# A state-space layer's kernel: the sums of two neighbouring sets made in one visit, and the order of its first stage written anew

## The chip, the cores and the metric

The kernel runs on one core of one Trainium2 chip. A core has five engines that each work through a list of instructions of their own: TensorE (PE in the profile; its weight loads are PEld), VectorE (DVE), ScalarE (ACT), GpSimd (POOL) and SyncE (SP, which here issues DMA transfers). They wait for one another by semaphores. The metric is the time of one execution on the device in microseconds (us), and lower is better. TensorE accumulates into PSUM, whose banks hold 512 numbers of 32 bits for each of 128 partitions in this kernel; the other tiles lie in SBUF, 128 partitions as well.

## The reference

One layer on 2048 tokens of 512 channels. `u` is normalised, then goes two ways: through a state-space convolution, and through an FFN (512 to 1792 to 512, GELU) whose output gates the first.

```python
xn = _layernorm(u)
# convolution: per channel d a kernel K[d, l] of 2048 taps, from 128 complex states
dt = exp(log_dt)[:, None];  logdA = dt * (A_re + 1j * A_im);  dB = dt * (B_re + 1j * B_im)
P = exp(logdA[:, :, None] * arange(L))
K = einsum("dn,dnl,dn->dl", C_re + 1j * C_im, P, dB).real
y = irfft(rfft(pad(xn)) * rfft(pad(K)))[:L] + xn * Dskip
# gate
h = gelu(einsum("bsd,df->bsf", xn, w1) + b1)
g = silu(einsum("bsf,fd->bsd", h, w2) + b2)
return u + y * g
```

## The kernel before

There are two stages. The first, up to about 394 us, is the projection stage: the layer norm, the whole FFN and the making of the kernel K. The second does the convolution as a transform in two steps with matmuls, and multiplies by the gate. The change lies in the first.

**The FFN** is 56 steps: eight passes of seven steps (four blocks of 512 tokens, each in two halves of the 1792 hidden rows). x, the weights and the hidden layer are each split in a high and a low part, and three products are summed: `first_half` (L243; L250 to L252) makes a hidden tile `f` in six matmuls a call, two calls a step; `gate` (L262) takes the GELU on ACT (`hf`); `gate_high` (L267) casts it to the high part `hh` on ACT; `ffn_rest` (L273) makes the low part `hl = hf - hh` on DVE; `second_part` (L279; L289 to L291) adds three products to one of four accumulators `z`, four calls a step. Weights are loaded by SP (`stage_first`, `stage_second`) and split by `split` (high parts on ACT, low parts `w1l`, `w2l` on DVE, L235, or on GpSimd). The layer norm's blocks are transposed by TensorE into `xT` (L361), into the buffers of `f` where the token is TF, and split by ACT and DVE into `xh` and `xl` (L376).

**The kernel K** is made in 32 sets of 16 channels. For each set `gen_phase` (L593) computes the angles of half the set by one matmul into `ph` (one bank), twice; `gen_round` (on ACT, L601, or on DVE, L603, by a flag) and `gen_wrap` (DVE, L607) reduce them to one turn in `ra`; `gen_size` (GpSimd, L616 and L619) builds the magnitudes `mm` by repeated products; `gen_sin` (ACT, L627 to L630) takes sine and cosine; `gen_tables` (DVE, L642 to L649) multiplies them into the tables `e1` and `e2`, which have two buffers each; `gen_sum` (L657) contracts e1 with e2 over the 128 states on PE, 32 small matmuls (64 records in the profile) into one half of the bank `kg`; `gen_out` copies it on ACT to `ko` (two buffers); `gen_keep` stores it by SP to `kgd`.

**What sets the order.** A table written out by hand, `ORDER`, is read token by token (the loop at L1101): each token names one of the actions above with its arguments, and calling it appends its instructions to the engines' lists. So an engine does its own instructions in the table's order, and between engines only semaphores decide. F.5.0 is first_half of step 5, its first half; G, H, R, S are gate, gate_high, ffn_rest and second_part; A, B, C, Z, N, E, Q, U, UD are gen_phase, gen_round, gen_wrap, gen_size, gen_sin, gen_tables, gen_sum, gen_out, gen_keep, the first number being the set (B with a third argument runs on the other engine); KL loads a set's inputs; W, WB and WS load and split the weights of a step; P is one step in the preparation of the parameters; TF, TH, TL transpose and split a block; D loads `dsk` and `fc` for the second stage.

Of the kernel before, what the change touches and what calls it, by code (L numbers as in the profile page):

```python
# [53 lines left out]
LS.4.0 B.0.0.1 TH.2.1 TL.2.0 C.0.0 WS.6.0 S.2.2 S.2.3 H.4 TF.3.0 A.0.1 KL.1.1 WS.5.2 S.3.0 LS.5.1 WS.6.1
Z.0 B.0.1 P.0 P.1 TH.3.0 S.3.1 C.0.1 S.3.2 A.1.0 N.0.0 TL.2.1 S.3.3 KL.2.0 LD.2 TL.3.0 WS.6.2 B.1.0.1
C.1.0 R.4 F.5.0 TF.3.1 Z.1 LD.3 LS.4.1 N.0.1 A.1.1 B.1.1.1 F.5.1 S.4.0 WS.5.3.1 TH.3.1.1 C.1.1 G.5 S.4.1
E.0.0 S.4.2 S.4.3 E.0.1 TL.3.1 F.6.0 H.5 N.1.0 R.5 F.6.1 LR.4 N.1.1 F.7.0 E.0.2 G.6 A.2.0 B.2.0.1 S.5.0
KL.2.1 LC.5 H.6 F.7.1 S.5.1 P.1 LC.4 C.2.0 WS.6.3 LK.0 F.8.0 S.5.2 A.2.1 G.7 KL.3.0 H.7 B.2.1 P.1 F.8.1
R.6 G.8 KL.3.1 C.2.1 N.2.0 S.5.3 F.9.0 E.1.0 N.2.1 Q.0 A.3.0 S.6.0 S.6.1 S.6.2 F.9.1 Z.2 E.1.1 R.7 U.0
E.1.2 P.1 LD.5 B.3.0.1 LD.4 C.3.0 O.0.0 TF.4.0 KL.4.0 Q.1 Z.3 O.0.1 H.8 S.6.3 TH.4.0 O.0.3 G.9 A.3.1  # L60
S.7.0 TL.4.0 B.3.1.1 P.1 H.9 S.7.1 C.3.1 O.0.2 KL.4.1 TF.4.1 UD.0 LL.6 TH.4.1 R.8 F.10.0 F.10.1 E.2.0
S.7.2 S.7.3 N.3.0 E.2.1 A.4.0 TL.4.1 P.1 S.8.0 R.9 KL.5.0 U.1 E.2.2 N.3.1 B.4.0.1 G.10 OK.0 S.8.1 F.11.0
E.3.0 F.11.1 S.8.2 C.4.0 A.4.1 S.8.3 Q.2 G.11 B.4.1 H.10 UD.1 TF.5.0 E.3.1 E.3.2 LK.1 F.12.0 H.11 TH.5.0
C.4.1 A.5.0 KL.6.0 LS.6.0 F.12.1 B.5.0.1 S.9.0 S.9.1 R.10 N.4.0 G.12 S.9.2 TL.5.0 TF.5.1 P.1 N.4.1 C.5.0
KL.5.1 S.9.3 F.13.0 A.5.1 U.2 TH.5.1 F.13.1 R.11 S.10.0 P.1 B.5.1 Z.4 P.1 P.1 Q.3 C.5.1 N.5.0 TL.5.1
S.10.1 P.1 E.4.0 P.1 UD.2 U.3 F.14.0 N.5.1 H.12 E.4.1 S.10.2 KL.6.1 UD.3 S.10.3 R.12 E.4.2 Z.5 G.13 A.6.0
S.11.0 S.11.1 F.14.1 H.13 LK.2 E.5.0 R.13 E.5.1 LL.7 S.11.2 S.11.3 B.6.0.1 C.6.0 Q.4 Z.6 S.12.0 G.14
A.6.1 KL.7.0 F.15.0 E.5.2 P.1 S.12.1 LS.7.0 B.6.1 LS.7.1 F.15.1 P.2 C.6.1 S.12.2 A.7.0 S.12.3 G.15 LS.6.1
F.16.0 B.7.0 C.7.0 LR.6 N.6.0 A.7.1 S.13.0 LC.6 KL.8.0 S.13.1 U.4 H.14 R.14 P.1 H.15 F.16.1 N.6.1 LC.7
P.2 UD.4 E.6.0 B.7.1 R.15 S.13.2 LD.6 KL.7.1 C.7.1 F.17.0 Z.7 S.13.3 F.17.1 G.16 TF.6.0 O.1.0 O.1.2 Q.5  # L70
A.8.0 E.6.1 G.17 TF.7.0 S.14.0 TH.6.0 P.2 TH.7.0 E.6.2 O.1.1 U.5 O.1.3 H.16 KL.8.1 TL.6.0 TL.7.0 B.8.0
N.7.0 Z.8 S.14.1 S.14.2 N.7.1 S.14.3 F.18.0 OK.1 UD.5 C.8.0 TF.6.1 A.8.1 P.2 Q.6 F.18.1 S.15.0 B.8.1.1
R.16 TH.6.1 S.15.1 C.8.1 S.15.2 U.6 KL.9.0 S.15.3 E.7.0 H.17 E.7.1 S.16.0 W.7 S.16.1 G.18 WB.7 A.9.0
KL.9.1 F.19.0 F.19.1 R.17 E.7.2 B.9.0 TL.6.1 N.8.0 S.16.2 W.8 LD.7 S.16.3 N.8.1 G.19 S.17.0 TF.7.1 C.9.0
A.9.1 E.8.0 P.2 H.18 KL.10.0 TH.7.1 E.8.1 Q.7 B.9.1.1 UD.6 C.9.1 KL.10.1 H.19 D S.17.1 S.17.2 A.10.0
E.8.2 S.17.3 N.9.0 WB.8 F.20.0 TL.7.1 P.2 F.20.1 U.7 KL.11.0 N.9.1 R.18 Z.9 B.10.0 S.18.0 C.10.0 E.9.0
A.10.1 Q.8 G.20 F.21.0 XL.0 W.9 S.18.1 B.10.1 C.10.1 KL.12.0 N.10.0 E.9.1 N.10.1 WB.9 S.18.2 E.9.2 R.19
S.18.3 W.10 F.21.1 A.11.0 F.22.0 U.8 B.11.0 C.11.0 S.19.0 KL.11.1 G.21 H.20 S.19.1 A.11.1 S.19.2 UD.7
Z.10 B.11.1 P.2 P.2 F.22.1 UD.8 LK.3 S.19.3 R.20 F.23.0 WB.10 G.22 C.11.1 E.10.0 N.11.0 S.20.0 Z.11
A.12.0 F.23.1 N.11.1 S.20.1 Q.9 H.21 O.2.0 S.20.2 E.10.1 E.10.2 B.12.0 KL.12.1 F.24.0 H.22 C.12.0 A.12.1  # L80
# [1126 lines left out]
```

## Time and profile before

| | us |
|---|---|
| median of three runs | 548.02 |
| lowest and highest run | 547.81, 549.68 |
| the profiled execution | 548.29 |
| its span, first to last instruction | 546.5 |
| PE, DVE, ACT, POOL busy in it | 526.9, 463.9, 394.5, 279.1 |

The span is divided among the engines, and every row of the profile is a group of instructions of one line: its engine, what it writes and reads, its count, the busy time in all and the mean of one, and the idle time ahead with what ended it. Busy times of the engines overlap. Matmuls are pipelined: one lasts longer than the time until the next starts, so what a piece of PE's work costs is read from the starts in the timeline. The granted clock of TensorE stands in the tables by stretch, 1.00 being full speed; its mean over the span is 0.996.

### The profile page before, as it was taken

To read this page: it belongs to the slowest core of one execution; us is meant where nothing else is said; L and a number is where in the kernel's file an instruction comes from. 1 tells how busy PE (TensorE), PEld (TensorE's weight loads), DVE (VectorE), ACT (ScalarE), POOL (GpSimd) and SP (SyncE) were. 2 spreads that over 40 slices of the span, in tenths; PEclk is the share of its full clock that TensorE was granted. 3 is DMA by queue.
4 is the path that set the end of the run, shared out by engine and by line. 5 is a ranking of instruction groups with operands and counts; after the bars stand their busy time and mean duration, and the time that the engine had idled before them with its cause. 6 is when DMAs were issued, how large, how long until landed. Compare 5 with 4: busy or idle time off the path is not lost.

```text
span 546.5 us, 16626 instructions
## 1 busy us (share of the span) xinstructions
PE 526.9 (96%) x6999; PEld 421.2 (77%) x6999; DVE 463.9 (85%) x736; ACT 394.5 (72%) x570; POOL 279.1 (51%) x385
## 2 busy tenths in 40 slices
PE   8898999999999999999999999999999999999993
PEld 7666787778776777777777777777789998997971
DVE  6899989999999889999888797789557688787896
ACT  3777998898987899959799777889664573652430
POOL 5648379358968559996854296356301001203031
PEclk9999999999999999999999999999999999999998
DMA  8937526744385172837038412913547749361562
GB/s 228 315 124 227 196 83 221 237 150 146 121 245 180 33 237 90 270 102 198 18 110 263 123 47 84 188 45 103 204 160 221 136 127 189 120 194 67 182 208 93
DMA packets 88391, 85.85 MB, mean 157 GB/s; under 512 B 42134, under 2 KB 65050, under 8 KB 87292
## 3 DMA queue, kind: packets, MB, share of 16 engines
q1 hardware_dynamic: 79248, 66.43, 41.6%
q0 software_dynamic: 8768, 17.83, 10.6%
q8 instruction: 55, 0.90, 0.7%
q10 hardware_dynamic: 300, 0.53, 0.3%
q14 instruction: 20, 0.16, 0.1%
HBM read 51.22 MB, written 33.55 MB: 155 GB/s over the span
## 4 chain that ended last, share of the span: by engine, by line
PE 76%; DVE 17%; issue 2%; ACT 1%; POOL 1%; DMA 1%; DVEq 0%; ACTq 0%; POOLq 0%
PE s L913 11%; PE z L289 8%; PE z L290 7%; PE z L291 7%; PE f L250 7%; PE f L252 7%; PE f L251 7%; PE s L891 6%; PE sa L949 6%; PE kg L657 5%; PE ph L593 2%; DVE hl L276 2%; DVE ra L607 2%; DVE e L646 1%; PE y L989 1%
## 5 line engine op out<-in xcount | busy, mean ns | idle before, releaser
L619 POOL TENSOR_TENSOR mm<-mm,rc 128x32 f32<-128x32 f32 (+4 forms) x150 | 115.4, 769 | 11.8
L289 PE MATMUL z<-w2h,hh 128*128 128x512 f32 x224 | 97.8, 437 | 0.0
L250 PE MATMUL f<-xh,w1h 128*128 128x512 f32 x220 | 91.4, 416 | 0.0
L291 PE MATMUL z<-w2h,hl 128*128 128x512 f32 x224 | 88.4, 395 | 0.3 <-DVE hl L276 0.3
L252 PE MATMUL f<-xh,w1l 128*128 128x512 f32 x220 | 87.1, 396 | 1.7 <-DVE w1l L235 1.7
L290 PE MATMUL z<-w2l,hh 128*128 128x512 f32 x224 | 88.6, 395 | 0.0
L251 PE MATMUL f<-xl,w1h 128*128 128x512 f32 x220 | 86.7, 394 | 0.0
L913 PE MATMUL s<-X,mc 64*64 64x128 f32 x1536 | 60.4, 273 | 0.2 <-issue 0.2
L930 DVE TENSOR_TENSOR t<-s,uh 128x512 f32<-128x512 f32 x64 | 41.0, 684 | 22.8 <-ACT uh L921 22.6
L276 DVE TENSOR_TENSOR hl<-hf,hh 128x512 fp32r<-128x512 f32 x56 | 52.9, 948 | 4.6 <-ACT hh L270 4.6
L616 POOL COPY mm<-rc 128x32 f32<-128x32 f32 x30 | 13.4, 446 | 77.7 <-DVE e L649 53.4
L264 ACT ACTIVATE hf<-f,b1s 128x512 f32<-128x512 f32 x56 | 38.2, 688 | 20.4 <-DVE hl L276 11.7
L252 PEld LDWEIGHTS f<-xh,w1l 128*128 128x128 f32 x220 | 41.3, 188 | 12.9 <-DVE w1l L235 3.0
L289 PEld LDWEIGHTS z<-w2h,hh 128*128 128x128 f32 x224 | 42.5, 190 | 10.5 <-issue 1.0
L291 PEld LDWEIGHTS z<-w2h,hl 128*128 128x128 f32 x224 | 42.1, 188 | 10.7 <-DVE hl L276 0.7
L607 DVE SCALAR_TENSOR_TENSOR ra<-ra,ph 128x512 f32<-128x512 f32 x64 | 43.6, 681 | 7.5 <-ACT ra L601 6.5
L913 PEld LDWEIGHTS s<-X,mc 64*64 64x64 f32 x1536 | 44.5, 133 | 5.8 <-issue 1.7
L290 PEld LDWEIGHTS z<-w2l,hh 128*128 128x128 f32 x224 | 42.3, 189 | 8.3 <-DVE w2l L235 0.2
L250 PEld LDWEIGHTS f<-xh,w1h 128*128 128x128 f32 x220 | 41.5, 189 | 9.2 <-ACT hf L264 0.2
L251 PEld LDWEIGHTS f<-xl,w1h 128*128 128x128 f32 x220 | 41.4, 188 | 9.0
L921 ACT COPY uh<-s 128x512 f32<-128x512 f32 x32 | 18.7, 586 | 38.3 <-PE s L913 18.4
L642 DVE TENSOR_TENSOR e<-mm,ra 128x1024 f32<-128x1024 f32 x32 | 42.0, 1311 | 4.7 <-POOL pr_h L524 2.4
(184 smaller groups left out, 1161.1 us busy)
## 6 DMA issues: line engine op xcount, KB each, us to landing
x<-in_A_u_dram SPq DMA_DIRECT2D x8, 512.0 KB
xs<-x SPq DMA_DIRECT2D x8, 512.0 KB
xt_h<-xh POOLq DMA_DIRECT2D x4, 1024.0 KB, 5.5
xt_l<-xl POOLq DMA_DIRECT2D x4, 1024.0 KB, 7.6
kgd<-ko SPq DMA_DIRECT2D x32, 128.0 KB
za<-zo SPq DMA_DIRECT2D x4, 1024.0 KB
xh<-xt_h POOLq DMA_DIRECT2D x4, 1024.0 KB, 6.1
xl<-xt_l POOLq DMA_DIRECT2D x4, 1024.0 KB, 10.1
```

What stands on the lines that cost most here:

```text
L250: PE.matmul(p, wh[:, k, :], xh[:, k, :], start=(k == 0), stop=False)
L251: PE.matmul(p, wh[:, k, :], xl[:, k, :], start=False, stop=False)
L252: PE.matmul(p, wl[:, k, :], xh[:, k, :], start=False, stop=(k == KD - 1))
L276: V.tensor_sub(hl, hf, hh)
L289: PE.matmul(z, hh[:, s], wh, start=(f0 == 0 and not rows), stop=False)
L290: PE.matmul(z, hh[:, s], wl, start=False, stop=False)
L291: PE.matmul(z, hl[:, s], wh, start=False, stop=(f0 == FA - 1))
L607: V.scalar_tensor_tensor(ra[:, 0, c], ra[:, 1, c], MAGIC, p, op0=ALU.subtract, op1=ALU.subtract)
L619: GP.tensor_mul(mv[:, :, 0:3:2, w:2 * w], mv[:, :, 0:3:2, 0:w], rc[:, 2 + 2 * i:4 + 2 * i, :].rearrange("p j c -> p c j").unsqueeze(3).to_ ...
L642: V.tensor_mul(e1, m1.unsqueeze(1).to_broadcast([P, 2, CH, N1]), ra[:, :, :, :N1])
L913: PE.matmul(p[ka * 64:(ka + 1) * 64, r, o, :, jj], w, xf[b][h, c, :, k, :], start=(c == 0), stop=(c == 1), skip_group_check=True)
L930: V.tensor_mul(t, p[:, i, :, 1].unsqueeze(1).to_broadcast([P, 2, 2, P]), uh)
```

## The change

1. `gen_sum` is called for odd sets only and does the sums of sets s-1 and s in one visit of 64 matmuls, into one full bank. `gen_out` copies 128 x 512 at once, `gen_keep` stores both sets in one transfer of 256 KB, and `ko` is one buffer of twice the size in place of two. The number of matmuls is the same. `e1` and `e2` keep two buffers each.
2. `ORDER` is replaced as a whole. Beside the order, 24 of the 64 roundings change their engine, so that 29 are on DVE (35 before) and 35 on ACT (29 before); ACT loads its function tables 59 times where it loaded them 66 times. The loads of D come earlier on SP, ahead of the weights of step 4.

```diff
 ORDER = """
-F.2.0 P.0 F.2.1 H.1 WS.3.0 R.1 WS.3.1 P.0 S.1.0 WS.3.2 WB.4 G.2 P.0 WS.4.0 S.1.1 W.5 WS.3.3 P.0 H.2
...
+W.3 WB.3 WS.3.0 F.2.1 WS.3.1 D WS.3.2 W.4 WB.4 W.5 P.0 WS.4.0 P.0 WS.3.3 WS.4.1 P.0 P.0 F.3.0 F.3.1 G.2
+H.2 P.0 WB.5 S.1.0 G.3 H.3 P.0 W.6 WS.4.2 LR.2 R.2 S.1.1 P.0 S.1.2 S.1.3 F.4.0 F.4.1 S.2.0 S.2.1 G.4
+WS.5.0 LC.2 TF.2.0 TF.2.1 TH.2.0 TH.2.1 H.4 S.2.2 LS.5.0 S.2.3 WS.5.1 WS.4.3.1 LC.3 KL.0.0 KL.0.1 TL.2.0
...
     def gen_size(s):
         rc = gen[s]["rc"]
         if s == 0:
-            for n in range(2):
-                GP.memset(par.tile([P, DD, N2], F32, tag="ko", name=f"ko_{n}", bufs=2)[:, 0, :1], 0.0)
+            GP.memset(par.tile([P, 2, DD, N2], F32, tag="ko", name="ko_")[:, 0, 0, :1], 0.0)
...
     def gen_sum(s):
-        e1, e2 = gen[s]["e"]
-        p = pss.tile([P, DD, N2], F32, tag="sm", name=f"kg{s}")
-        for d in range(DD):
-            for c in range(2):
-                for g in range(G):
-                    PE.matmul(p[g * N1:(g + 1) * N1, d, :], e1[:, c, g * DD + d, :], e2[:, c, g * DD + d, :],
-                              start=(c == 0), stop=(c == 1), skip_group_check=True)
+        p = pss.tile([P, 2, DD, N2], F32, tag="sm", name=f"kg{s}")
+        for n in range(2):
+            e1, e2 = gen[s - 1 + n]["e"]
+            for d in range(DD):
+                for c in range(2):
+                    for g in range(G):
+                        PE.matmul(p[g * N1:(g + 1) * N1, n, d, :], e1[:, c, g * DD + d, :], e2[:, c, g * DD + d, :],
+                                  start=(c == 0), stop=(c == 1), skip_group_check=True)
         gen[s]["p"] = p
 
     def gen_out(s):
-        gen[s]["ko"] = ko = par.tile([P, DD, N2], F32, tag="ko", name=f"ko{s}", bufs=2)
+        gen[s]["ko"] = ko = par.tile([P, 2, DD, N2], F32, tag="ko", name=f"ko{s}")
         A.copy(ko, gen[s]["p"])
 
     def gen_keep(s):
-        b, j = divmod(s, SPB)
-        SY.dma_start(kgd[b][:, j * DD * N2:(j + 1) * DD * N2], gen.pop(s)["ko"].rearrange("p a b -> p (a b)"))
+        b, j = divmod(s // 2, SPB // 2)
+        SY.dma_start(kgd[b][:, j * 2 * DD * N2:(j + 1) * 2 * DD * N2], gen.pop(s)["ko"].rearrange("p n a b -> p (n a b)"))
```

In the changed kernel's listing lines from L230 to L612 stand two lower and from L642 to L663 some three lower, since the table is two lines shorter. How instructions stand now is shown at three places. In a row the line comes first, then the operation, the tile written and the tiles read with a number of their own, and the size; `x32` is 32 of the same kind.

First, PE at the sum of set 20, before:

```order
L289 MATMUL z5_0_3521<-w2h10_2718,hh_5_10_3627 128x512
L290 MATMUL z5_0_3521<-w2l10_2719,hh_5_10_3627 128x512
L291 MATMUL z5_0_3521<-w2h10_2718,hl_5_10_3638 128x512
L657 MATMUL kg20_3753<-e2_20_3553,e1_20_3552 32x64 x32
L250 MATMUL f1_6_7_3802<-xh_2_3275,w1h7_2475 128x512
L251 MATMUL f1_6_7_3802<-xl_2_3276,w1h7_2475 128x512
L252 MATMUL f1_6_7_3802<-xh_2_3275,w1l7_2476 128x512
```

In the changed kernel, PE where sets 20 and 21 are summed (`ph23`, `ph24` are the angles of sets 23 and 24, `z5` and `f1_6` belong to the FFN):

```order
L287 MATMUL z5_3_3469<-w2h11_2741,hh_5_11_3677 128x512
L288 MATMUL z5_3_3469<-w2l11_2742,hh_5_11_3677 128x512
L289 MATMUL z5_3_3469<-w2h11_2741,hl_5_11_3679 128x512
L591 LDWEIGHTS lh23_3574
L591 MATMUL ph23_1_3781<-cbs_122,lh23_3574 128x512
L655 MATMUL kg21_3788<-e2_20_3644,e1_20_3643 32x64 x32
L655 MATMUL kg21_3788<-e2_21_3672,e1_21_3671 32x64 x32
L591 LDWEIGHTS lh24_3753
L591 MATMUL ph24_0_3856<-cbs_122,lh24_3753 128x512
L248 MATMUL f1_6_8_3763<-xh_2_3687,w1h8_2519 128x512
```

The sum of 20, which stood by itself between FFN matmuls, now waits for the tables of 21, and stands with that of 21 between two angle matmuls.

Second, DVE at the same place before, from the tables of set 21 (`e1_21`, `e2_21`) to those of set 22:

```order
L646 TENSOR_TENSOR e2_21_3728<-mm21_3703,ra21_3512 128x32x32
L276 TENSOR_TENSOR hl_5_11_3739<-hf_5_11_3640,hh_5_11_3721 128x512
L642 TENSOR_TENSOR e1_22_3788<-mm22_3741,ra22_3668 128x1024
L276 TENSOR_TENSOR hl_5_12_3825<-hf_5_12_3684,hh_5_12_3725 128x512
L648 TENSOR_TENSOR e2_21_3728<-mm21_3703,ra21_3512 128x16x32
L649 SCALAR_TENSOR_TENSOR e2_21_3728<-mm21_3703,ra21_3512 128x16x32
L603 TENSOR_SCALAR ra23_3840<-ph23_0_3812 128x512
L607 SCALAR_TENSOR_TENSOR ra23_3840<-ra23_3840,ph23_0_3812 128x512
L646 TENSOR_TENSOR e2_22_3789<-mm22_3741,ra22_3668 128x32x32
```

and in the changed kernel:

```order
L643 TENSOR_TENSOR e2_21_3672<-mm21_3476,ra21_3424 128x32x32
L645 TENSOR_TENSOR e2_21_3672<-mm21_3476,ra21_3424 128x16x32
L646 SCALAR_TENSOR_TENSOR e2_21_3672<-mm21_3476,ra21_3424 128x16x32
L274 TENSOR_TENSOR hl_5_12_3776<-hf_5_12_3681,hh_5_12_3683 128x512
L601 TENSOR_SCALAR ra23_3778<-ph23_0_3761 128x512
L605 SCALAR_TENSOR_TENSOR ra23_3778<-ra23_3778,ph23_0_3761 128x512
L605 SCALAR_TENSOR_TENSOR ra23_3778<-ra23_3778,ph23_1_3781 128x512
L639 TENSOR_TENSOR e1_22_3858<-mm22_3712,ra22_3674 128x1024
L643 TENSOR_TENSOR e2_22_3859<-mm22_3712,ra22_3674 128x32x32
```

The four operations that make the tables of one set now stand closer together: all of set 21's lie ahead of the first of set 22, which follows on three operations on the angles of set 23 (`ra23`). Before, the first of set 22 stood ahead of the last two of set 21.

Third, PE at the beginning, the FFN's steps 0 and 1 of the first block, before:

```order
L251 MATMUL f1_0_1_350<-xl0_271,w1h1_327 128x512
L252 MATMUL f1_0_1_350<-xh0_270,w1l1_328 128x512
L288 MATMUL z0_0_373<-b2r_123,ones_124 128x512
L289 MATMUL z0_0_373<-w2h0_250,hh_0_0_367 128x512
L290 MATMUL z0_0_373<-w2l0_251,hh_0_0_367 128x512
L291 MATMUL z0_0_373<-w2h0_250,hl_0_0_369 128x512
L289 MATMUL z0_1_374<-w2h0_250,hh_0_0_367 128x512
L290 MATMUL z0_1_374<-w2l0_251,hh_0_0_367 128x512
L291 MATMUL z0_1_374<-w2h0_250,hl_0_0_369 128x512
L250 MATMUL f1_0_1_350<-xh0_270,w1h1_327 128x512
```

and in the changed kernel:

```order
L249 MATMUL f1_0_1_359<-xl0_271,w1h1_329 128x512
L250 MATMUL f1_0_1_359<-xh0_270,w1l1_330 128x512
L248 MATMUL f1_0_1_359<-xh0_270,w1h1_329 128x512
L249 MATMUL f1_0_1_359<-xl0_271,w1h1_329 128x512
L250 MATMUL f1_0_1_359<-xh0_270,w1l1_330 128x512
L248 MATMUL f1_0_1_359<-xh0_270,w1h1_329 128x512
L249 MATMUL f1_0_1_359<-xl0_271,w1h1_329 128x512
L250 MATMUL f1_0_1_359<-xh0_270,w1l1_330 128x512
L286 MATMUL z0_0_372<-b2r_123,ones_124 128x512
L287 MATMUL z0_0_372<-w2h0_250,hh_0_0_350 128x512
L288 MATMUL z0_0_372<-w2l0_251,hh_0_0_350 128x512
L289 MATMUL z0_0_372<-w2h0_250,hl_0_0_357 128x512
```

Both halves of step 1 (`f1_0_1`) now stand ahead of the first row that reads `hl_0_0`; before, the second half came after two rows of the accumulators.

More of the change, by code (lines that the diff above doesn't have):

```diff
@@ L54 @@
[L54 to L68, printed above, removed]
@@ new lines @@
+ZA.0.1 A.21.0 B.21.0.1 H.36 S.34.2 S.34.3 KL.22.0 KL.21.1 F.39.0 H.37 Z.20 F.39.1 C.21.0 A.21.1 N.20.1
+S.35.0 S.35.1 Z.21 Q.19 ZA.0.3 KL.22.1 ZA.0.2 R.36 B.21.1.1 R.37 C.21.1 A.22.0 P.3 S.35.2 G.38 N.21.0
+KL.23.0 S.35.3 S.36.0 S.36.1 S.36.2 S.36.3 P.3 G.39 H.38 ZG.0 SL1.3 F.40.0 N.21.1 S.37.0 S.37.1 U.19
+UD.19 F.40.1 F.41.0 F.41.1 E.20.0 P.3 ZD.0 KL.23.1 S.37.2 S.37.3 R.38 S.38.0 E.20.1 E.20.2 E.21.0
+B.22.0.1 C.22.0 H.39 R.39 G.40 H.40 G.41 XL.2 A.22.1 B.22.1.1 P.3 F.42.0 S.38.1 C.22.1 P.3 Z.22 S.38.2
@@ L128 @@
+B.30.1.1 ZA.2.3 C.30.1 ST N.30.0 F.53.1 H.51 E.29.0 E.29.1 E.29.2 S.49.2 S.49.3 A.31.0 R.51 KL.31.1 G.52
+B.31.0.1 C.31.0 H.52 Z.30 S.50.0 R.52 S.50.1 S.50.2 S.50.3 S.51.0 G.53 A.31.1 B.31.1 C.31.1 Q.29 S.51.1
+S.51.2 S.51.3 N.30.1 E.30.0 UD.27 U.29 N.31.0 N.31.1 KL0 F.54.0 UD.29 H.53 E.30.1 E.30.2 Z.31 F.54.1
+ZG.2 G.54 E.31.0 E.31.1 E.31.2 SL1.2 R.53 F.55.0 F.55.1 ZD.2 S.52.0 S.52.1 S.52.2 Q.31 U.31 S.52.3 H.54
+S.53.0 S.53.1 G.55 H.55 UD.31 S.53.2 S.53.3 R.54 R.55
 """
```

127 lines of the change are left out of this document (64 added, 63 removed).

## The prediction

> **What bounds the kernel now.** I read the page's first part, then the stretches, then what TensorE (PE) waits for. The page's first part and a table by stretch (start and end, length, then busy time of PE, weight load, DVE, ACT and POOL with instruction counts, granted clock, DMA share, GB/s):
>
> ```profile
> PE 526.9 (96%) x6999; PEld 421.2 (77%) x6999; DVE 463.9 (85%) x736; ACT 394.5 (72%) x570; POOL 279.1 (51%) x385
> ...
> 0.00:50.00 50.00, 42.44 (x211) 33.53 (x212) 43.22 (x104) 31.30 (x59) 31.26 (x71) 1.00 0.72 226
> 50.00:390.00 340.00, 338.07 (x3297) 260.63 (x3296) 305.18 (x431) 294.26 (x393) 223.88 (x289) 1.00 0.50 146
> 390.00:546.50 156.50, 146.43 (x3495) 126.99 (x3493) 115.46 (x203) 68.97 (x119) 23.96 (x27) 0.98 0.55 158
> ```
>
> The change rewrites the order of the stage that ends near 390 us. There PE has 338.07 of 340 us: it is the bound, and the other engines matter only where they make it wait. DVE has 340 - 305.18 = 34.8 us to spare, ACT 45.7. The clock is 1.00, so no gain or loss comes from it. In the second stage, from about 394 us, no instruction changes but the loads that precede it: I take it as it is.
>
> What PE waits for, over the whole span (us in total, times, longest):
>
> ```profile
> PE ph L593 <- DVE ra L607: 2.2, 4, 0.9
> PE xT L361 <- DVE xl L376: 1.8, 1, 1.8
> PE f L252 <- DVE w1l L235: 1.7, 2, 1.5
> ...
> PE xT L361 <- ACT hf L264: 0.9, 2, 0.6
> ...
> PE z L291 <- DVE hl L276: 0.3, 1, 0.3
> ```
>
> Of these only `ph` waits beyond 50 us, 1.9 of its 2.2. So a better order can win in the first 50 us and hardly elsewhere, and what else can go is PE work.
>
> **The merged sums.** Around one summing visit of before (start, duration, instruction; an L291 matmul ahead, three of the FFN behind):
>
> ```profile
> 99.43 0.40 PE L290 MATMUL z<-w2l,hh 128*128 128x512 f32 x1
> 99.67 0.39 PE L291 MATMUL z<-w2h,hl 128*128 128x512 f32 x1
> 99.98 1.10 PE L657 MATMUL kg<-e,e 128*32 128x64 f32 x64
> 101.01 0.50 PE L289 MATMUL z<-w2h,hh 128*128 128x512 f32 x1
> 101.35 0.40 PE L290 MATMUL z<-w2l,hh 128*128 128x512 f32 x1
> 101.58 0.39 PE L291 MATMUL z<-w2h,hl 128*128 128x512 f32 x1
> ```
>
> FFN matmuls start 0.24 us apart (99.43 to 99.67) though each lasts 0.40: starts, not durations, tell what something costs. Entry into the visit took 0.31 (99.67 to 99.98), 0.07 to 0.08 over that cadence; exit 0.34 (101.01 to 101.35), 0.10 to 0.11 over it; the 64 records between took 1.03. The same 64 records per set remain; entry and exit, 0.19 together, are paid 16 times instead of 32: 16 x 0.19 = **-3.0 us**. Least: if only the exit is saved, 16 x 0.11 = -1.8. Most: where a sum stands right ahead of a `ph`, the exit costs nothing (69.44 then 69.48 below), and by the two orders seven of the new visits stand so against five of the old: 3.04 + 2 x 0.11 = -3.3.
>
> ```profile
> 68.41 1.10 PE L657 MATMUL kg<-e,e 128*32 128x64 f32 x64
> 69.44 0.39 PE L593 MATMUL ph<-cbs,lh 96*128 96x512 bf16 x1
> 69.48 0.58 PE L289 MATMUL z<-w2h,hh 128*128 128x512 f32 x1
> ```
>
> **The other engines' savings.** On ACT 32 copies of 361 ns become 16 of twice the width; the nearest row for that width is 586 ns.
>
> ```profile
> L663 ACT COPY ko<-kg x32: 345/364/376, 71.4 to 392.3; 128x256 f32<-128x256 f32 x32
> L921 ACT COPY uh<-s 128x512 f32<-128x512 f32 x32 | 18.7, 586 | 38.3 <-PE s L913 18.4 <-issue 10.2 <-ACT Z L960 7.3
> L264 ACT ACT_TABLE_LOAD x29 | 37.2, 1283 | 1.6 <-DVE hl L276 1.1
> L603 DVE TENSOR_SCALAR ra<-ph 128x512 f32<-128x512 f32 x35 | 24.0, 685 | 12.8 <-PE ph L593 11.9
> ```
>
> That is 32 x 0.364 - 16 x 0.586 = 2.3 us less. Seven table loads fewer (66 to 59 by the two orders) at 1.283 are 9.0 less; six roundings `ra` that move from DVE to ACT are 6 x 0.685 = 4.1 less on DVE and, at the same price, as much more on ACT. ACT then has 7.2 us less, DVE 4.1 less. Worth to the end: **0**, since PE covers both over 340 us; with the cover gone (every PE wait on DVE beyond 50 us) the most it returns is the 1.9 us above. SP issues 16 stores fewer, of twice the size. The loads of token D (four of `dsk`, one of `fc`) now stand ahead of w1s4 on SP; I cost them at 0, because w1l4's only trace on PE is the 0.14 us at 35.23 below; if the five issues push w1s4 late, the bound is another w1l wait like the longest one, +1.5.
>
> **The first 50 us.** PE's rows there where a start comes late:
>
> ```profile
> 17.41 0.40 PE L251 MATMUL f<-xl,w1h 128*128 128x512 f32 x1
> 19.32 0.50 PE L252 MATMUL f<-xh,w1l 128*128 128x512 f32 x1 [1.52 <-DVE w1l L235]
> ...
> 20.82 0.40 PE L290 MATMUL z<-w2l,hh 128*128 128x512 f32 x1
> 21.52 0.50 PE L291 MATMUL z<-w2h,hl 128*128 128x512 f32 x1 [0.29 <-DVE hl L276]
> ...
> 30.22 0.40 PE L251 MATMUL f<-xl,w1h 128*128 128x512 f32 x1
> 30.80 0.50 PE L252 MATMUL f<-xh,w1l 128*128 128x512 f32 x1 [0.17 <-DVE w1l L235]
> ...
> 34.86 0.40 PE L251 MATMUL f<-xl,w1h 128*128 128x512 f32 x1
> 35.23 0.50 PE L252 MATMUL f<-xh,w1l 128*128 128x512 f32 x1
> ...
> 38.81 0.63 PE L361 MATMUL xT<-ident,x 128*128 128x128 f32 x4 [0.28 <-ACT hf L264]
> ...
> 40.92 0.66 PE L361 MATMUL xT<-ident,x 128*128 128x128 f32 x4 [0.57 <-ACT hf L264]
> ...
> 44.75 0.66 PE L361 MATMUL xT<-ident,x 128*128 128x128 f32 x4 [1.77 <-DVE xl L376]
> ```
>
> Against the cadence of 0.23 the four FFN rows lose 1.68, 0.47, 0.35 and 0.14. The first stays: the order on PE up to there is the same and it waits for w1l1, whose operations come in the same order. The second goes, since six more matmuls of F.1.1 (1.4 us) now stand ahead of the row that waits for `hl`. The third and fourth I let go as well, since the splits of blocks 2 and 3 stand earlier against PE's visits: 0.96 in all. The waits of the three `xT` are 0.28 + 0.57 + 1.77 = 2.62. In the new order the first two transposes stand together behind S.2.1, whose two buffers (`hf` of steps 3 and 4) were read earlier; the third still needs the buffer that `xl` frees. I let about half go, 1.3. Together **-2.2**; least 0, if w1l and `xl` are as late against PE as before; most 0.96 + 2.62 = -3.6.
>
> **The later waits.** This is the term that only an order decides. Per set DVE must give PE `ra` twice, and PE's next `ph` into the one bank waits for it. With four `ph` waits of 2.2 / 4 = 0.55 us mean in the trace, and in the new order the tightest places (around sets 8 to 12, 18, 22 to 24) tighter, I add two: **+1.1**. Least -1.9, if those beyond 50 us go too; most 16 x 0.9 = +14.4, one wait as long as the longest row at each pair.
>
> Sum: -3.0 - 2.2 + 1.1 = -4.1. The rows are of an execution of 548.29 us (span 546.5), 0.27 above the median of 548.02; I make the sum against the execution: 548.29 - 4.1 = **544.2 us**.
>
> **Rivals.** (a) Nothing that a measurement can tell from no change, which for this kernel is about 0.5%, 2.7 us (545.3 to 550.8). The merge holds, the first 50 us keep their waits (DVE has 43.22 of 50 there, so a new order may only move them), and the later waits grow by 1.1: 548.29 - 3.0 + 1.1 = 546.4. For it: before has only two us of waits to lose beyond 50. Against it: 0.96 of the early ones fall by the mere order of rows.
>
> (b) Slower: a new wait of DVE on the paired sum. `e1` and `e2` have two buffers, so before, e of set 22 had to wait for the sum of 20 alone; now it waits for the visit that reads 20 and 21. In the order shown, `ph23_1`, both sums and `ph24_0` follow one another on PE, and `e1_22` stands right behind `ra23` on DVE. From the start of `ph23_1`: the visit ends after 0.23 + 0.08 + 2.06 + 0.1, some 2.45 us. DVE gets there after `ph` 0.38, a rounding on ACT, taken at the 0.685 of L603, and the wrap, 0.681 by the row here: 1.75.
>
> ```profile
> L607 DVE SCALAR_TENSOR_TENSOR ra<-ra,ph 128x512 f32<-128x512 f32 x64 | 43.6, 681 | 7.5 <-ACT ra L601 6.5
> L276 DVE TENSOR_TENSOR hl<-hf,hh x56: 659/855/2370, 20.8 to 389.9; 128x512 fp32r<-128x512 f32 x56
> L276 DVE TENSOR_TENSOR hl<-hf,hh 128x512 fp32r<-128x512 f32 x56 | 52.9, 948 | 4.6 <-ACT hh L270 4.6
> L646 DVE TENSOR_TENSOR e<-mm,ra x32: 1210/1307/2134, 55.2 to 383.7; 128x1024 f32<-128x1024 f32 x32
> L646 DVE TENSOR_TENSOR e<-mm,ra 128x1024 f32<-128x1024 f32 x32 | 45.2, 1412 | 0.0
> ```
>
> So DVE stands for 0.7 us at such a pair; at 16 pairs 11.2. What queues behind it on DVE are the next `e`, `hl` and `ra`, and PE waits for those. If all of it reaches PE: 544.2 + 11.2 = 555.4. It decides when more than 4.1 / 0.7, about six of the sixteen pairs, pass their wait on; against it stand DVE's 34.8 us of idle time.
>
> (c) Much faster: VectorE and GpSimd really come apart. The rows above show `hl` at 659 ns at best and 948 in the mean, `e` of L646 at 1210 and 1412: 56 x 0.289 + 32 x 0.202 = 22.7 us of DVE time. Then every wait of PE on DVE can go, 2.2 + 1.8 + 1.7 + 0.3 = 6.0 us, and the sum is 548.29 - 3.0 - 6.0 = 539.3. More is not there, as PE has no more to wait for. Against it: POOL's 223.88 us and DVE's 305.18 are together 189 over the 340, so that 189 of POOL's lie beside DVE whatever the order, and each engine starts an instruction when its inputs are there, not when the table would have it.
>
> The Trainium skill ("SBUF — State Buffer", section "Who interferes with whom") says that VectorE and GpSimd share a pair of ports as an exclusive lock, and that a VectorE instruction with two inputs in SBUF contends with a GpSimd instruction that reads SBUF. `hl` and `e` are such instructions, and their spread agrees with it. By that rule alone the way out is (c), and the stretched `hl` would fall toward 659.
>
> **How the numbers follow.** My forecast 0.42, (a) 0.20, (b) and other new waits of that kind 0.27, (c) 0.11. The forecast's own range is 541.5 to 547. The 80% range runs from (c)'s 539.5 to 553, which takes in three quarters of (b): 12 of 16 pairs, 544.2 + 8.4 = 552.6. Faster by over 0.5% (under 545.3): most of the forecast, 0.39, and (c), 0.11: 0.50. Within 0.5%: (a) and what the forecast leaves, 0.23. Slower: 0.27.
>
> **What the changed profile would show.** Merge: 16 visits of 128 records, each about 2.06 from its first start to the next matmul's, with entry and exit as above. Early waits: no `hl` row near 21.5, one or two `xT` waits under 1 us, the 1.5 us at 19.3 still there; the stretch before 50 us some 2 us further on. Later: `ph` waiting for `ra` about six times. (b) shows as DVE idle at L639 (the first `e`) released by PE's sum, and as PE waits on `hl` and `ra`. (c) shows as `hl` below 800 ns in the mean and DVE's busy time some 20 us less. I am wrong if PE's waits between 50 and 390 exceed 6 us, or if `hl` gets longer, not shorter.

## The result, and the profile after

| | before | changed |
|---|---|---|
| median, us | 548.46 | 543.61 |
| lowest to highest | 547.81 to 549.68 | 541.98 to 544.24 |
| runs | 4 | 4 |
| profiled execution | 548.29 | 544.24 |
| its span | 546.5 | 542.4 |

The ratio is 0.9904 with a 95% interval of 0.9875 to 0.9933: faster by 0.96%, 4.9 us in the medians and 4.05 between the two profiled executions. The forecast was 544.2.

The changed kernel's busy times by engine, and its three stretches, in the form shown of the kernel before:

```profile
PE 522.2 (96%) x6999; PEld 421.9 (78%) x6999; DVE 456.7 (84%) x730; ACT 389.5 (72%) x553; POOL 274.6 (51%) x384
...
0.00:50.00 50.00, 44.46 (x224) 36.19 (x225) 43.60 (x106) 32.50 (x60) 29.54 (x66) 1.00 0.73 225
50.00:390.00 340.00, 335.89 (x3378) 262.31 (x3378) 298.58 (x423) 288.45 (x377) 223.58 (x295) 1.00 0.50 147
390.00:542.40 152.40, 141.83 (x3405) 123.43 (x3401) 114.50 (x202) 68.56 (x118) 21.43 (x24) 0.98 0.58 162
```

In the first 50 us PE is busy 2.0 us longer than before; between 50 and 390 it is idle 4.1 us where it was idle 1.9. So the new order won time at the beginning and lost as much later; what is left must be PE's own work. A double summing visit that stands alone between FFN matmuls shows it (start, duration, instruction):

```profile
314.25 0.40 PE L249 MATMUL f<-xl,w1h 128*128 128x512 f32 x1
314.49 0.39 PE L250 MATMUL f<-xh,w1l 128*128 128x512 f32 x1
314.81 1.99 PE L655 MATMUL kg<-e,e 128*32 128x64 f32 x128
316.74 0.50 PE L287 MATMUL z<-w2h,hh 128*128 128x512 f32 x1
317.07 0.40 PE L288 MATMUL z<-w2l,hh 128*128 128x512 f32 x1
```

From the last FFN start ahead (314.49) to the second behind (317.07) are 2.58 us, of which two steps of the cadence, 0.23 to 0.24 each, would pass anyway: the visit costs 2.12. The single one shown in the prediction takes 101.35 - 99.67 = 1.68, less the same 0.46: 1.22. Two single visits cost 2.45 (twice 1.223 before rounding), the double one 2.12: 0.33 saved each time, and 16 x 0.33 = 5.2 us in all. Not every visit stands alone between FFN matmuls; reckoned in the same way from the starts of all of them, the 32 visits of before cost 37.4 us and the 16 of the changed kernel 31.7, which is 5.6 less.

What PE waits for between 50 and 402 us in the changed kernel, and the one wait of DVE that its list puts down to the sums:

```profile
PE pT L559 <- DVE ra L605: 1.6, 1, 1.6
PE ph L591 <- DVE ra L605: 1.6, 3, 0.8
PE z L287 <- DVE zo L391: 0.4, 1, 0.4
PE f L248 <- ACT hf L262: 0.2, 1, 0.2
PE z L287 <- ACT zo L389: 0.2, 1, 0.2
...
DVE e L639 <- PE kg L655: 1.1, 1, 1.1
```

That is 4.0 us against 1.9. In the first 50 us the FFN, transposes and angles waited 1.52 + 0.29 + 0.17 + 0.28 + 0.57 + 1.77 + 0.30 = 4.90 us before (the rows shown in the prediction, and 0.30 of `ph` at 48.1); now these are left (idle time in brackets):

```profile
19.37 0.50 PE L250 MATMUL f<-xh,w1l 128*128 128x512 f32 x1 [1.54 <-DVE w1l L233]
35.35 0.50 PE L250 MATMUL f<-xh,w1l 128*128 128x512 f32 x1 [1.05 <-DVE w1l L233]
40.23 0.63 PE L359 MATMUL xT<-ident,x 128*128 128x128 f32 x4 [0.45 <-DVE x L343]
42.44 0.66 PE L359 MATMUL xT<-ident,x 128*128 128x128 f32 x4 [0.18 <-DVE xl L374]
```

3.2 us, so 1.7 less. (In the second profile of the same kernel, e5 below, they are 3.7, so 1.2 less.) The sum by rows is -5.2 - 1.7 + 2.1 = -4.8, or -5.2 with the 5.6. The last FFN matmul starts at 402.1 where it started at 407.0 (the first rows of the two fences below, before and changed, give first and last starts), 4.9 earlier, which lies between the two. Behind it the second stage took 542.4 - 402.1 = 140.3 where it took 139.5: 0.8 is given back there, and -4.1 is left. In e5's execution of the same kernel it took 139.8, so the 0.8 is not shown to be the change's doing.

```profile
L291 PE MATMUL z<-w2h,hl x224: 387/395/497, 21.5 to 407.0; 128*128 128x512 f32 x112
```

```profile
L289 PE MATMUL z<-w2h,hl x224: 387/396/478, 22.5 to 402.1; 128*128 128x512 f32 x112
L274 DVE TENSOR_TENSOR hl<-hf,hh 128x512 fp32r<-128x512 f32 x56 | 49.8, 895 | 4.9 <-ACT hh L268 4.9
L639 DVE TENSOR_TENSOR e<-mm,ra 128x1024 f32<-128x1024 f32 x32 | 43.6, 1364 | 4.9 <-PE z L289 2.8 <-PE kg L655 1.1 <-POOL mm L613 0.7
L643 DVE TENSOR_TENSOR e<-mm,ra 128x1024 f32<-128x1024 f32 x32 | 43.4, 1358 | 0.0
```

The last three rows are DVE's `hl` and first two table operations: 895 ns in the mean where it was 948, 1364 where it was 1311, 1358 where it was 1412. VectorE's operations have not come clear of GpSimd's.

### The profile page after: what moved, and what is told of

It is laid out like the page before. It is cut to its first block, busy times and chain, and to the rows that moved or that the text cites. A ratio compares the mean times of both kernels' runs of the same rounds, so it can differ in the third digit from the quotient of the medians.

```text
span 542.4 us, 16557 instructions
## 1 busy us (share of the span) xinstructions
PE 522.2 (96%) x6999; PEld 421.9 (78%) x6999; DVE 456.7 (84%) x730; ACT 389.5 (72%) x553; POOL 274.6 (51%) x384
## 4 chain that ended last, share of the span: by engine, by line
PE 70%; DVE 20%; ACT 3%; DMA 3%; issue 2%; SPq 0%; POOL 0%; DVEq 0%; ACTq 0%
PE s L911 10%; PE z L287 7%; PE z L288 7%; PE z L289 7%; PE f L248 6%; PE f L250 6%; PE f L249 6%; PE s L889 6%; PE sa L947 5%; PE kg L655 4%; DVE e L639 2%; PE ph L591 2%; DVE e L643 2%; DVE hl L274 2%; PE y L987 1%
## 5 line engine op out<-in xcount | busy, mean ns | idle before, releaser
L616 POOL TENSOR_TENSOR mm<-mm,rc 128x32 f32<-128x32 f32 (+4 forms) x150 | 106.1, 708 | 11.8
L287 PE MATMUL z<-w2h,hh 128*128 128x512 f32 x224 | 95.7, 427 | 0.6 <-DVE zo L391 0.4
L274 DVE TENSOR_TENSOR hl<-hf,hh 128x512 fp32r<-128x512 f32 x56 | 49.8, 895 | 4.9 <-ACT hh L268 4.9
L605 DVE SCALAR_TENSOR_TENSOR ra<-ra,ph 128x512 f32<-128x512 f32 x64 | 43.7, 682 | 11.2 <-ACT ra L599 10.2
L639 DVE TENSOR_TENSOR e<-mm,ra 128x1024 f32<-128x1024 f32 x32 | 43.6, 1364 | 4.9 <-PE z L289 2.8
```

Source lines behind the costliest of these rows:

```text
L274: V.tensor_sub(hl, hf, hh)
L287: PE.matmul(z, hh[:, s], wh, start=(f0 == 0 and not rows), stop=False)
L605: V.scalar_tensor_tensor(ra[:, 0, c], ra[:, 1, c], MAGIC, p, op0=ALU.subtract, op1=ALU.subtract)
L616: GP.tensor_mul(mv[:, :, 0:3:2, w:2 * w], mv[:, :, 0:3:2, 0:w], rc[:, 2 + 2 * i:4 + 2 * i, :].rearrange("p j c -> p c j").unsqueeze(3).to_ ...
L639: V.tensor_mul(e1, m1.unsqueeze(1).to_broadcast([P, 2, CH, N1]), ra[:, :, :, :N1])
```

## The experiments

Each time is told with the time of the kernel before on the same chip, and compared by the ratio. Line numbers differ by some lines from kernel to kernel; the tiles' names are the same.

**The merge in the old order** (e1). The new functions, the old table without the even sets' sums, copies and stores. Where the tables of the next set stood ahead of the paired sum, one of the two had to move, since the tables have two buffers:

```diff
-... Q.0 ... U.0 ... UD.0 ... (all even sets)
-E.6.0 ... Q.5          (also sets 7, 9, 19, 25)
+Q.5 E.6.0
-E.12.0 E.12.1 ... Q.11
+Q.11 E.12.0 E.12.1
-E.22.0 ... E.22.1 ... Q.21
+Q.21 E.22.0 E.22.1
```

> The order of before with the merged sums alone: the even sets' sums, copies and stores are left out of the table, the odd sets' make both; where the first tables of the next set stood ahead of the paired sum, the sum moves ahead of them (five places) or they behind it (two places). Theory A (from the starts inside the visits after the change: 64 records more in one visit take 0.893 us, and a visit alone costs 1.223, so each visit has a fixed 0.33 us): 548.4 - 16 x 0.33 = 543.2. Rival B (the prediction's 0.19 per visit): 545.4. Rival C (the gain is the new order's): 547 or more.

Measured 561.02 against 548.78, ratio 1.0223 (1.0196 to 1.025). Rival C's "547 or more" takes it in, but no theory had such a size: the merge placed so makes the kernel 12 us slower. The visits are as short as in the changed kernel (a double one alone costs 2.1), so their 5.2 us are there. The waits of DVE and of PE between 50 and 420 us tell the rest:

```profile
DVE e L635 <- PE kg L651: 21.5, 11, 4.9
...
PE ph L587 <- DVE ra L601: 13.6, 12, 3.2
```

DVE stands 21.5 us at eleven places until a paired sum has read the tables that it wants to write over, and behind it the wraps `ra` come late, for which PE waits 13.6 us, against 1.9 in that stretch before. The longest place, in DVE's list, and the sum that it waits for in PE's:

```profile
346.42 0.97 DVE L270 TENSOR_TENSOR hl<-hf,hh 128x512 fp32r<-128x512 f32 x1
352.31 1.23 DVE L635 TENSOR_TENSOR e<-mm,ra 128x1024 f32<-128x1024 f32 x1 [4.93 <-PE kg L651]
353.46 0.68 DVE L601 SCALAR_TENSOR_TENSOR ra<-ra,ph 128x512 f32<-128x512 f32 x1
...
351.08 1.99 PE L651 MATMUL kg<-e,e 128*32 128x64 f32 x128
```

The wrap that PE needs next stands right behind the waiting table operation. That operation starts 1.23 us after the visit's first record, when the visit still has some 0.7 us to go: it needs only the first half, which reads the even set. So DVE does not wait for a longer visit; it waits because the even set's sum now comes no earlier than the odd set's.

PE's waits account for 12.2 us more than before (13.6 + 0.3 + 0.2 against 1.9). Behind two of them, of 3.24 and 1.93 us, the granted clock also fell to one half for some 3.4 us each (start and end, length, busy time of PE, weight load, DVE, ACT and POOL with counts, granted clock, DMA share, GB/s):

```profile
153.20:156.20 3.00, 3.00 (x8) 2.33 (x8) 2.62 (x5) 2.97 (x5) 0.00 (x0) 0.50 0.00 0
385.60:388.60 3.00, 3.00 (x9) 2.32 (x8) 2.12 (x4) 2.97 (x4) 2.48 (x6) 0.51 0.00 0
```

That is another 3.4 us of PE's time, and the two make 15.6 of the 17 us that were lost beside the merge's 5.2; the rest was not found. This is the prediction's rival (b), at more than the 11.2 us that it was priced at: it is avoided by the new order, not by slack that was there. (A third buffer for the tables might take the wait away; it was not tried, nor was another placing of the paired sums in the old order.)

**The new order without the merge** (e2). The visits are parted, the bank stays:

```diff
 def gen_sum(s):
+    n = s % 2
+    if n == 0:
+        gen["sm"] = pss.tile([P, 2, DD, N2], F32, tag="sm", name=f"kg{s}")
+    p = gen["sm"]
-    for n in range(2):
-        e1, e2 = gen[s - 1 + n]["e"]
+    e1, e2 = gen[s]["e"]
...
 (table: Q of each even set put between two FFN entries some way ahead of Q of the odd one)
```

> The new order, with each double visit parted again: the even set's 64 records go by themselves between two FFN matmuls some way ahead, into the other half of the same bank; copy, store and all else stay. Theory A: 543.6 + 16 x 0.33 = 548.8. Rival B: 543.6 + 16 x 0.19 = 546.6. Rival D (the visits lie in time that PE waits away anyway): 543.6 to 544.5. If DVE's wait on the paired sum (tables with two buffers) costs PE anything, this kernel gets some of it back.

Measured 551.85 against 548.78, ratio 1.0059 (1.0041 to 1.0077), some 8.4 us above the changed kernel by the ratios. Theory A's visits are in the trace, a lone one again at 1.24 (256.59 to 258.29 less 0.46):

```profile
256.59 0.40 PE L285 MATMUL z<-w2h,hl 128*128 128x512 f32 x1
256.92 1.10 PE L653 MATMUL kg<-e,e 128*32 128x64 f32 x64
257.95 0.50 PE L283 MATMUL z<-w2h,hh 128*128 128x512 f32 x1
258.29 0.39 PE L284 MATMUL z<-w2l,hh 128*128 128x512 f32 x1
```

So 5.2 of the 8.4 are the fixed cost of sixteen more visits, more than B's 3.0. For the other 3 the profile has more than is needed, since the profiled execution, 553.89, is the slowest of the eleven: PE waits 5.2 us beyond 50 (4.0 in the changed kernel) and 0.5 longer in the first 50, and the second stage takes 2.4 longer, though nothing was moved in these two; why they grew stays open. With e1 this makes a table of four kernels, each by its ratio to before:

| | sums single | sums paired |
|---|---|---|
| old order | 1 | 1.0223 |
| new order | 1.0059 | 0.9907 |

Neither part is a gain alone, as placed here. The new order is made for paired sums, and paired sums need it.

**The old beginning** (e3). The first 122 entries of the table are those of the old order, the others follow in the new one.

```diff
-P.0 P.0 WS.0.3 WS.1.0 P.0 LD.0 WS.1.1 ... (new table)
+WS.0.3 LD.0 LD.1 P.0 WS.1.0 WS.1.1 P.0 ... S.3.3 KL.2.0 LD.2 (old table), then the new one's remaining entries
```

> The first 122 entries of the table (about the first 50 us) in the order of before, the rest in the new order. Theory: the early waits of PE (about 5.7 us before, 4.4 after by the starts beyond the cadence) return: 543.6 + 1.4 = 545.0. The prediction's term: 543.6 + 2.2 = 545.8. Rival: the two beginnings are worth the same, 543.6.

Measured 547.41 against 548.78, ratio 0.997 (0.9954 to 0.9985): the new beginning is worth (0.997 - 0.9907) x 548.4 = 3.5 us, above the prediction's 2.2 and not nothing. The old waits are back, the last of them longer than it was:

```profile
21.59 0.50 PE L285 MATMUL z<-w2h,hl 128*128 128x512 f32 x1 [0.32 <-DVE hl L270]
30.86 0.50 PE L246 MATMUL f<-xh,w1l 128*128 128x512 f32 x1 [0.16 <-DVE w1l L229]
38.90 0.63 PE L355 MATMUL xT<-ident,x 128*128 128x128 f32 x4 [0.30 <-ACT hf L258]
40.99 0.66 PE L355 MATMUL xT<-ident,x 128*128 128x128 f32 x4 [0.55 <-ACT hf L258]
45.57 0.66 PE L355 MATMUL xT<-ident,x 128*128 128x128 f32 x4 [2.53 <-DVE xl L370]
```

With the 1.5 us at 19.4, which the changed kernel has as well, these make 5.4 us against 3.2. Behind the last and longest the granted clock fell to one half, as in e1:

```profile
46.90:50.10 3.20, 3.20 (x10) 2.20 (x8) 3.17 (x7) 1.90 (x3) 3.12 (x6) 0.50 0.44 172
```

That is another 1.6 us of PE's time. It was lost in this execution; the mean clock of the twelve lies between 0.990 (this one) and 0.995, so not in each of them. In the two profiles of the changed kernel, and in that of the kernel before, the clock is 1.00 from the start to the end of the FFN.

**The changed kernel once more** (e5), on the chip of the following runs.

> The changed kernel once more, on the chip of the next three, so that they are compared with it and not only with the kernel before. Ratio to before 0.990 as measured, between 0.988 and 0.993.

543.09 against 548.39, ratio 0.9907 (0.9894 to 0.992). In its profile the early rows wait 1.53 + 1.34 + 0.34 + 0.52 = 3.7 us (3.2 in the first profile), the later ones 3.7 (4.0), and the last FFN matmul starts at 402.4 (402.1).

**Later sums** (e6). Nothing but FFN entries put ahead of eight of the paired sums:

```diff
-Q.7 ... S.17.0 ... S.17.1
+S.17.0 S.17.1 Q.7
```

> The changed kernel with eight of the sixteen paired sums put one or two FFN entries later on PE (15 entries of 0.7 or 1.4 us, 13 us of delay in all); nothing else moves. It doses the wait that cost the old order its gain. If the new order hides the wait by only a little slack: DVE's wait for the sums grows from 1.1 to 5 us or more and the time by 2 to 6 us. If the sums stand far ahead of where DVE needs them: no change, within 1 us of the changed kernel.

546.66 against 548.39, ratio 0.9971 (0.9954 to 0.9988): 3.5 us slower than the changed kernel, for 13 us of delay. Its runs lie between 544.66 and 548.36, and the profiled one is the lowest. In that one DVE waits 2.9 us for the sums at three places in place of 1.1 at one; the time moved as the theory of little slack said, though DVE's wait grew less than the 5 us expected of it, and the profile does not show where the slower runs lost theirs.

**No magnitudes on GpSimd** (e7, e10). In the changed kernel, and then in the kernel before, sets 2 to 31 use the magnitudes of sets 0 and 1, so that GpSimd's work on them is left out; all else stands.

```diff
 def gen_size(s):
+    if s > 1:
+        gen[s]["mm"] = gen["mm", s % 2]
+        return
```

> The changed kernel without the magnitudes of sets 2 to 31 on GpSimd (those of sets 0 and 1 are used again): some 100 us of GpSimd's work left out, nothing moved. If GpSimd's work stretches DVE's: hl falls from a mean of 895 ns toward its least, 657, the tables from about 1364 toward 1210, DVE's busy time by 15 to 30 us. For the time: the theory that PE is the bound gives at most PE's waits on DVE in the changed kernel, 2.6 + 1.6 + 1.6 + 0.6, so 538 to 541; the rival, that separation is worth nothing more now, 543.6.

> The kernel before without the magnitudes of sets 2 to 31 on GpSimd (those of sets 0 and 1 are used again), as was done to the changed one, where it gave 4.8 us (543.1 to 538.3). If the new order's gain is that it keeps GpSimd's work off DVE's, the kernel before must gain more, 7 us or over: 541 or less. If not, it gains as much or less: 543.5 or more, and the two orders differ by what they do with PE's visits.

The changed kernel: 538.32 against 548.39, ratio 0.9818 (0.9802 to 0.9834), 4.9 us less than with them. The kernel before: 545.88 against 548.21, ratio 0.9953 (0.9935 to 0.9971), 2.6 us less. The changed kernel without them, by engine, and its `hl`, first table operation and wrap:

```profile
PE 519.4 (97%) x6999; PEld 420.7 (78%) x6999; DVE 423.8 (79%) x730; ACT 389.0 (72%) x553; POOL 109.9 (20%) x174
...
L270 DVE TENSOR_TENSOR hl<-hf,hh 128x512 fp32r<-128x512 f32 x56 | 40.3, 725 | 5.6 <-ACT hh L264 5.5
L638 DVE TENSOR_TENSOR e<-mm,ra 128x1024 f32<-128x1024 f32 x32 | 39.2, 1229 | 8.3 <-ACT ra L626 7.6 <-PE kg L654 0.7
...
L601 DVE SCALAR_TENSOR_TENSOR ra<-ra,ph 128x512 f32<-128x512 f32 x64 | 43.8, 685 | 19.8 <-ACT ra L595 18.9
```

With 165 us of GpSimd's work gone, DVE has 33 us less to do with the same instructions: `hl` falls from 895 to 725 ns, the table from 1364 to 1229. The wrap `ra<-ra,ph`, which has one input in PSUM, keeps its time: 681 ns before, 682 in the changed kernel, 685 here. PE waits for nothing between 50 and 390 us, in this kernel (the first row) or in the kernel before without its magnitudes (the second):

```profile
50.00:390.00 340.00, 340.00 (x3430) 266.74 (x3430) 267.77 (x427) 290.59 (x381) 59.61 (x86) 1.00 0.52 151
50.00:390.00 340.00, 340.00 (x3341) 262.53 (x3343) 271.65 (x431) 295.45 (x394) 54.71 (x80) 1.00 0.50 147
```

So GpSimd's neighbourhood costs DVE 33 us, more than the 30 expected at most, and GpSimd's work costs PE 4.9. (DVE's one wait of 0.7 us for the magnitudes goes as well, so not all of the 4.9 need come from the stretched operations.) In the kernel before DVE's busy time falls as much, from 463.9 to 429.5, but the time by only 2.6, less than the 7 that "kept apart" asked for (the three of its five executions whose mean clock is not under 0.994 give the same, 545.68 in the median): the old order lost less of PE's time to GpSimd than the new one does, and the change's gain is not that the two engines were separated. The pair is also a second measure of the change without its later waits: (0.9953 - 0.9818) x 548.3 = 7.4 us, of which the merge's 5.2 to 5.6 and the beginning's 1.2 to 1.7 make most. The Trainium skill ("SBUF — State Buffer", section "Who interferes with whom") says that VectorE instructions with two inputs in SBUF contend with GpSimd's reads; `hl` and `e` are of that kind, and their fall to 725 and 1229 agrees, as does the unchanged time of the wrap, which is not.

**Three tries at PE's remaining waits** (e4, e8, e9).

```diff
 e4
-WS.4.0 P.0 WS.3.3 ... WS.4.2      -E.2.0 F.11.0 F.11.1 B.3.1 KL.4.1 C.3.1      -E.12.1 ... C.13.1
+WS.4.0 P.0 WS.3.3 WS.4.2          +F.11.0 F.11.1 B.3.1 KL.4.1 C.3.1 E.2.0      +C.13.1 E.12.1
 e8
-KL.3.1 P.1 ... C.3.1 ... N.3.1 P.1 ... C.4.0      -E.12.1 ... C.13.1
+KL.3.1 ... C.3.1 P.1 ... N.3.1 ... C.4.0 P.1      +C.13.1 E.12.1
 e9
-A.5.1 P.1 P.1 F.13.0 N.4.1 E.4.0 B.5.1 C.5.1      -E.12.1 ... C.13.1
+A.5.1 F.13.0 N.4.1 B.5.1 C.5.1 P.1 P.1 E.4.0      +C.13.1 E.12.1
```

> The changed kernel with three entries moved, each off DVE's way to a wait of PE: the low part of w1 of step 4 goes ahead of the parameters' steps (PE waits 1.05 for it near 35 us); the first tables of set 2 go behind the wrap of set 3 (PE waits 1.65 near 102 us); the second tables of set 12 go behind the wrap of set 13 (0.85 near 193 us). If these waits are real and nothing stands behind them: 543.6 - 1.05 - 1.2 - 0.85 = 540.5. Rival: another wait takes their place, 542.6 to 543.6.

544.94 against 548.78, ratio 0.9926 (0.9905 to 0.9947), no better than the changed kernel. The wait near 35 us is gone, and two on `hl` stand in its place, 1.5 us in all: what is put ahead on DVE pushes something else behind. The second move was aimed at the wrong sets, as e9's expectation says.

> The changed kernel with the parameters' last DVE step and its transpose (sets 8 to 15 need them long after) moved behind the wraps of sets 3 and 4, so that PE's 1.65 us near 102 us have no cause left, and the second tables of set 12 behind the wrap of set 13 (0.6 of 0.85 us gone when that was moved before). 543.6 - 1.65 - 0.6 = 541.3; if another wait takes the place, 543 to 544.

548.17 against 548.39, ratio 1.0001 (0.9989 to 1.0012): the whole gain lost by three moved entries. What the first of them carried was not the last step of the parameters but six short operations ahead of it. PE's wait at the parameters' transpose grew from 1.65 to 4.31 us, which is 2.7 of the 5.2 us lost against e5. Behind it the granted clock fell to one half:

```profile
106.60:112.20 5.60, 5.60 (x15) 4.12 (x16) 4.95 (x8) 5.00 (x5) 2.29 (x4) 0.50 1.00 306
```

PE loses 2.8 us there, and the two together are the loss. The mean clock of all twelve executions, 0.989 to 0.992, lies below that of the changed kernel's eight, 0.993 to 0.995.

> The changed kernel with two places of DVE's list altered: the wrap of set 5's second half goes ahead of the parameters' steps and of the first table of set 4 (in the trace it is this wrap, not that of set 3, that PE's 1.65 us near 102 us wait for; it was ready at 96.3 and ran at 101.8), and the second table of set 12 goes behind the wrap of set 13. If the wait is all there is: 543.1 - 1.65 - 0.6 = 540.9. If DVE has as little to spare as the other moves made it look, the steps put off make another wait: 543 or more.

543.86 against 548.21, ratio 0.992 (0.9898 to 0.9942), within the changed kernel's interval. Now the transpose `pT` comes without a wait, and PE stands four us later instead, for the same steps that were put off:

```profile
101.61 0.27 PE L555 MATMUL pT<-ident,pr_ar 128*128 128x128 f32 x1
101.72 0.27 PE L555 MATMUL pT<-ident,pr_ci 128*128 128x128 f32 x1
106.11 0.38 PE L587 MATMUL ph<-cbs,lh 96*128 96x512 bf16 x1 [2.01 <-DVE rec L558]
```

A wait of 1.65 became one of 2.01: here removing one of PE's waits only names the next.

## Why the prediction was right

**The bound.** PE was the bound, and stays it: 335.89 of 340 us between 50 and 390. The 11.3 us that ACT and DVE lost of their work by the forecast (7.2 and 4.1) were put at 0; DVE is 7.2 us less busy, ACT 5.0, and between 50 and 390 us PE waits longer than before, not shorter. "The clock is 1.00" holds for this stage in all three profiles of the two kernels, but it is no constant: e1, e3 and e8 lost 1.6 to 3.4 us by it.

**The merge was mis-sized**: -3.0 forecast, -5.2 measured. The step that failed is "the 64 records between took 1.03". That time runs from the first record's start to the start of the FFN matmul behind, and was taken whole for the records' own. The double visit shows that 64 more records add 2.12 - 1.22 = 0.90; the rest of the 1.03, some 0.13, is paid once a visit like the entry and the exit, and the bound of -3.3 was too near. The fixed cost of a visit is 0.33 us and not 0.19. The Trainium skill ("TensorEngine Tiling (Array Packing)", section "Key Properties") states that changing the tiling mode drains TensorE. The sums use 32 columns of the array where the FFN uses 128, and the 0.33 us agrees with a cost paid at each change, though no run here tells the drain from other causes.

**The early waits** were forecast at -2.2, and came at -1.7 by the rows, -1.2 by those of e5 and -3.5 by e3, where part is the clock. Of the single ones, the `hl` wait went and the 1.5 us at 19.3 stayed, as said. "The third and fourth I let go as well" was wrong of one: w1l of step 4 waits 1.05 us where it lost 0.14, since the parameters' steps stand ahead of it on DVE. The three `xT` waits fell from 2.62 to 0.63, further than the half that was counted.

**The later waits** were forecast at +1.1 and came at +2.1, and not by the mechanism that was given. "I add two" let `ph` wait six times for `ra`; it waits three times, 1.6 us in all, where before it waited three times beyond 50 us, 1.9. What grew lies at places that the prediction did not name: 1.6 us at the parameters' transpose behind the wrap of set 5, and 0.8 at three FFN rows. The sign was right by luck.

**The second stage** was taken as it is, and took 0.8 us longer in this profile, 0.3 in e5's.

So -5.2 - 1.7 + 2.1 + 0.8 = -4.0 stands against -3.0 - 2.2 + 1.1 + 0 = -4.1: the sum is right to a tenth because the merge's excess, the early waits' shortfall, the later waits' excess and the second stage cancel, which is luck. By the medians the change is worth 4.9.

**Rival (b)** was right as a mechanism, and wrong in its price and its condition. It let the next table operation wait for the whole visit, 2.45 us from the start of `ph23_1` (its four terms make 2.47), where DVE arrives after 1.75. In the changed kernel PE and DVE at that place, the pair 20 and 21:

```profile
297.57 0.39 PE L591 MATMUL ph<-cbs,lh 96*128 96x512 bf16 x1
297.89 1.99 PE L655 MATMUL kg<-e,e 128*32 128x64 f32 x128
299.82 0.39 PE L591 MATMUL ph<-cbs,lh 96*128 96x512 bf16 x1
...
298.72 0.69 DVE L605 SCALAR_TENSOR_TENSOR ra<-ra,ph 128x512 f32<-128x512 f32 x1 [2.33 <-ACT ra L599]
299.33 1.22 DVE L639 TENSOR_TENSOR e<-mm,ra 128x1024 f32<-128x1024 f32 x1
```

DVE arrives 299.33 - 297.57 = 1.76 us after the start of `ph23_1`, as worked out, and starts at once, half a us before the visit ends: the tables of 22 take the buffers of 20, which the visit's first half reads, and 64 records take about 1.0. So there is no wait of 0.7 us at such a pair. Of the waits of DVE only one, of 1.1 us, is put down to a sum, at 255 us, some forty us earlier; the sines of ACT that the same operation reads ended at 255.06, 0.04 before the sum, so even that one need not be the sum's.

"Against it stand DVE's 34.8 us of idle time" protects nothing: e1 has that idle time too, and lost 17 us beside the merge's 5.2. What protects the changed kernel is where the sums stand: the table operations of a set stand together ahead of the sum, and other work for DVE stands between the sum and the next tables. e6 agrees, in which later sums lose 3.5 us.

**Rival (c)** did not come, and its ceiling was about right: with GpSimd's magnitudes left out the time is 538.3, where 539.3 was worked out (the 80% range begins at 539.5).

## What to carry to other kernels

Measure what a burst of small matmuls costs by two bursts of different length, not by one: the time from its first start to the next instruction's still holds a part that is paid once a visit. Before two uses of a buffer are joined into one, ask how much later the first of them comes, which writer waits for it, and what stands behind that writer in its list: here that turned a gain of 5 us into a loss of 12 until the order was rewritten for it. When a list is nearly full, moving one operation off a wait can make the next, as in three tries here; leaving out work of the engine that slowed it did shorten the time. And look at the clock by fine stretches behind a long wait: a mean of 0.99 over a stage can hide it.

## What was not expected of the hardware

A visit of the 32-column sums costs 0.33 us beside its records, more than its entry and exit show. And the same instructions of DVE took 33 us longer in all (456.7 against 423.8) beside 165 us of GpSimd's work, about one us for every five, and 34 longer in the old order (463.9 against 429.5); but GpSimd's work cost PE's time only 2.6 us in the old order and 4.9 in the new.

Behind waits of PE of 1.93, 2.53, 3.24 and 4.31 us the granted clock fell to 0.50, for 3.2 to 5.6 us (e1, e3, e8). Behind the wait of 1.75 us near 44.6 us in e10 it fell too, from 45.8 to 49.0; behind the same wait in the kernel before, 1.77 us, it stayed at 1.00, as it did behind one of 2.4 in e2. So these traces do not tell what length of wait brings the fall about, nor that the wait alone does.
